# Linear attention and two MLPs on one core: the second MLP's output layer moved to Strassen's scheme

## The chip, the cores and the metric

The kernel runs on one core of a Trainium2 chip. The metric is the device time of one execution in microseconds, the median of several runs; lower is better. Beside the times there is one profiled execution, from which every row below is taken.

## The reference

All data are float32. The attention part and the first MLP come first and are not touched by the change.

```python
q_s = softmax(q, axis=-1); k_s = softmax(k, axis=2)      # 8 batches, 8 heads, 576 positions, 64 wide
x  = (q_s @ (k_s.T @ v)), laid out as 4608 tokens x 512
x  = square(relu(x @ moe_w_in)) @ moe_w_out              # 512 -> 2048 -> 512
h  = x @ moe2_w_in                                       # second MLP: 512 -> 2048
out = (h * sigmoid(1.702 * h)) @ moe2_w_out              # 2048 -> 512
```

## The kernel before

Every float32 matrix operand is cut into a high part (a ScalarE copy that rounds, `to_hi`) and a low part (a subtraction on GpSimd or VectorE, `to_lo`), and each product is three matmuls, hi·hi, hi·lo and lo·hi (`three`). The order of all instructions is written out by hand: a list `ORDER` for the start, and after it a `plan` of steps, each with a time, which is sorted by time. The times only set the order on each engine; semaphores do the rest. SP issues all DMAs, in the order of the plan.

The first MLP runs over 9 blocks of 512 tokens. Its output goes to DRAM (`y_d`). The second MLP runs over 6 blocks of 768 tokens (`NB2`), each block in 8 steps called quads (`NQ`), 256 of the 2048 hidden features per quad.

*First layer of a quad* (`steps_l1`): Strassen's scheme in Winograd's form, so seven products of half-size blocks instead of eight. Each product is 2 chunks x 3 = 6 matmuls with 384 moving columns. The seven forms of x (a11, s2, a12, s3, s1, a22, s4) are made once per block (`steps_s`). The seven forms of w_in live in SBUF for the whole second MLP (tiles w1, wa, wq, wbb, made by `steps_q`). The products accumulate in two PSUM banks (`pa`, `ps`); ScalarE copies the first (m1), VectorE adds m1 to the others (line 815), ScalarE applies the activation (line 824), and `to_hi` (line 134) and `to_lo` (line 137, GpSimd) make the four blocks `gc` of the hidden values.

*Second layer of a quad* (`unit`): plain, 12 units of 3 matmuls with 512 moving columns. The 128 x 128 stationary operand is a piece of the hidden values, the moving operand is a row block of w_out, and the sums of a block's six token tiles stay in six PSUM banks over its 8 quads:

```python
g, w = g_t["2", n, c], wt["o2", i, f]
cs = slice(t * P, (t + 1) * P)
three(acc, lambda e: g[:, e, cs], lambda e: w[:, e, :], len(seen) == 1, len(seen) == NF)
```

The units of quad n-1 stand between the products of quad n:

```python
UNITS = [0, 0, 1, 1, 2, 2, 3, 3, 4, 4, 5, 6]
...
                for e in range(2 if n >= NQ else 0):
                    at(quad(n) + (0.3 + 0.1 * e) * PT, load_o, n // NQ, 2 * (n % NQ) + e)
...
                for e, (c, t) in zip(UNITS, todo, strict=True):
                    at(quad(n) + (e + 0.47) * PT, unit, n - 1, c, t)
```

Two tiles of w_out per quad (512 KB each, hi and lo together) are loaded from DRAM (`wod`, line 712), where block 1 left them (`steps_o`). At the end of a block ScalarE and VectorE copy the banks (lines 899, 901) and six DMAs of 256 KB store 128 rows of 2 KB each (line 903).

Of the kernel before, what the change touches and what calls it, by code (L numbers as in the profile page):

```python
# [53 lines left out]
g15.re x10.s g15.sq g14.hi o15.hi g14.lo x11.s o15.lo x13.xh s13.all x13.xl g15.hi g15.lo  # L54
"""
# [3 lines left out]
def kernel(  # L59
# [54 lines left out]
    PT = QT / 7  # L114
# [28 lines left out]
    def at(t, fn, *args):  # L143
        plan.append((t, len(plan), fn, args))
# [7 lines left out]
    split_d = [dram.tile([P, 2, DM], F32, name=f"wod{f}") for f in range(NF)]  # L152
# [127 lines left out]

    def steps_o(n):
# [9 lines left out]
        def split(e):  # L291
            def run():
                f = 2 * n + e
                w = new_o(0, f)
                to_hi(w[:, 0, :], st["t"][:, e, :])
                to_lo(w[:, 1, :], st["t"][:, e, :], w[:, 0, :], nc.gpsimd)
                nc.sync.dma_start(out=split_d[f], in_=w.bitcast(F32))

            return run

        return dict(ld=load, s0=split(0), s1=split(1))

# [62 lines left out]
    def split_x(i, p):  # L365
# [339 lines left out]
    freed = [(t, f"{kind}{f}") for t, kind, f in freed]  # L705

    def new_o(i, f):
        wt["o2", i, f] = wpool.tile([P, 2, DM], F32R, tag=freed[-4:][f % 4][1], name=f"wo2_{i}_{f}")
        return wt["o2", i, f]

    def load_o(i, f):
        nc.sync.dma_start(out=new_o(i, f).bitcast(F32), in_=split_d[f])

    def steps_s(i):
# [25 lines left out]
        def split(a, src, eng):  # L740
            def run():
                x = xpool.tile([P, 2, 2, TH], F32R, tag=X_AT[a], name=f"{a}_{i}")
                to_hi(x[:, 0], src())
                to_lo(x[:, 1], src(), x[:, 0], eng)
                x_t["2", i, a] = x

            return run

        def s2():
            if i < 2:  # L750
                st["s2"] = block(0, 0)
            else:
                st["s2"] = cpool.tile([P, 2, TH], F32, tag="raw", name=f"s2f{i}")
            sub(st["s2"], st["s1"], block(0, 0), nc.vector if i < 2 else nc.gpsimd)

        def s4():
            sub(block(0, 0), block(0, 1), st["s2"])

        return dict(
            ld=load,  # L760
            s1=s1,
            s3=s3,
            s2=s2,
            a11=split("a11", lambda: block(0, 0), nc.gpsimd),
            s2s=split("s2", lambda: st["s2"], nc.vector),
            a12=split("a12", lambda: block(0, 1), nc.gpsimd),
            s4=s4,
            s3s=split("s3", lambda: block(1, 0), nc.vector),
            s1s=split("s1", lambda: st["s1"], nc.gpsimd),
            a22=split("a22", lambda: block(1, 1), nc.vector),  # L770
            s4s=split("s4", lambda: block(0, 0), nc.gpsimd),
        )

    def steps_l1(n):
# [5 lines left out]
        def product(at, x, begin):  # L780
            def run():
# [3 lines left out]
                w, xs = wt[a, j], x_t["2", i, x]  # L785
# [13 lines left out]
        def tile_(name):  # L799
            pool, tag = dict(  # L800
                m1=(late, "m1"), c12=(late, "c12"), c22=(late, "c22"), c21=(None, "t"), c11=(None, "t")
            )[name]
            pool = cpool if pool is None else late["pool"]
            return pool.tile([P, TH], F32, tag=tag, name=f"{name}_{n}", bufs=2 if tag in ("c12", "t") else 1)
# [23 lines left out]
        def split(name):  # L828
            def run():

                last = (name == "c12") == (n % 2 == 0) and name in ("c12", "c21")
                pool, tag = (late["pool"], "g4") if last else (gpool, "g")
                g = pool.tile([P, 2, TH], F32R, tag=tag, name=f"g{name}_{n}")
                to_hi(g[:, 0, :], st[name])
                to_lo(g[:, 1, :], st[name], g[:, 0, :], nc.gpsimd)
                g_t["2", n, name] = g
# [3 lines left out]
        return [  # L840
            (0.0, product(0, "a11", True)),
            (0.48, m1),
            (1.0, product(1, "s2", True)),
            (1.5, add("c12", 1, "m1")),
            (2.0, product(0, "a12", False)),
            (2.5, act("c11")),
            (3.0, product(1, "s3", False)),
            (3.1, split("c11")),
            (3.5, add("c22", 1, "m1")),
            (4.0, product(0, "s1", True)),  # L850
            (4.5, add("c22", 0, "c22")),
            (4.55, act("c22")),
            (5.0, product(1, "a22", False)),
            (5.1, split("c22")),
            (5.5, add("c21", 1, "m1")),
            (5.55, act("c21")),
            (6.0, product(0, "s4", False)),
            (6.1, split("c21")),
            (6.5, add("c12", 0, "c12")),
            (6.55, act("c12")),  # L860
            (7.1, split("c12")),
        ]

    def unit(n, c, t):

        i, j = divmod(n, NQ)
        if ("2", i) not in acc_t:
            acc_t["2", i] = {}
        tokens = (int(c[1]) - 1) * (NT2 // 2) + t
        f = 2 * j + int(c[2]) - 1  # L870
        if tokens not in acc_t["2", i]:
# [188 lines left out]
```

## Time and profile before

| | |
|---|---|
| median of 3 runs | 1652.45 us (1650.57 to 1653.61) |
| profiled execution, its own time | 1650.79 us |
| its span, first to last instruction | 1649.0 us |
| TensorE busy, share of the span | 99% |
| VectorE, ScalarE, GpSimd busy | 48%, 41%, 41% |
| DMA queue of SP, share of 16 engines | 29.5%, 158.37 MB |

Busy time of TensorE counts overlapping matmuls once. How long a stage takes is read from the start of one product to the start of the same product of the next quad. "PEld" is the load of the stationary operand, which overlaps with the matmul before it.

### The profile page before, as it was taken

What the parts mean: (1) busy time and instruction counts of PE and PEld (TensorE: products, weight loads), DVE (VectorE), ACT (ScalarE), POOL (GpSimd) and SP (SyncE); (2) the same over time, 40 slices, a digit from 0 to 9 for tenths busy, and PEclk for the clock granted to TensorE, in tenths of its full rate; (3) what the DMA queues carried; (4) which work ended last, traced back from release to release, by engine and by line L of the source; (5) the groups of instructions that cost most, each with busy time, mean ns of one, the idle gap of its engine ahead of it and who ended that gap; (6) DMA issues with size and microseconds to landing.
All of it is one profiled execution on the core that took longest, in us unless ns stands there. A gap on an engine that the chain in (4) does not pass through costs nothing.

```text
span 1649.0 us, 21337 instructions
## 1 busy us (share of the span) xinstructions
PE 1629.5 (99%) x7848; PEld 1404.4 (85%) x7848; DVE 789.8 (48%) x1455; ACT 673.2 (41%) x1228; POOL 684.0 (41%) x589
## 2 busy tenths in 40 slices
PE   6999999999999999999999999999999999999999
PEld 5888888888888888888888989889888898898987
DVE  8976777676776767656456113113113113113111
ACT  5874344444444444333435334324234234234332
POOL 4774333433433343343488445234234234234221
PEclk9999999999999999999999999999999999999999
DMA  8742233223323222121312334222222322321212
GB/s 241 236 141 73 73 106 84 81 87 100 100 68 108 82 63 86 61 77 52 103 44 90 141 113 143 90 77 101 104 77 85 120 78 77 128 76 72 96 61 81
DMA packets 127913, 159.74 MB, mean 97 GB/s; under 512 B 54080, under 2 KB 90944, under 8 KB 127808
## 3 DMA queue, kind: packets, MB, share of 16 engines
q1 hardware_dynamic: 127808, 158.37, 29.5%
q8 instruction: 62, 1.02, 0.2%
q14 instruction: 43, 0.35, 0.1%
HBM read 122.68 MB, written 35.65 MB: 96 GB/s over the span
## 4 chain that ended last, share of the span: by engine, by line
PE 91%; DVE 5%; issue 2%; DMA 1%; SPq 1%; ACT 1%; POOL 0%; DVEq 0%; POOLq 0%; ACTq 0%
PE acc L627 45%; PE ph L627 21%; PE ps L627 15%; PE pa L627 6%; PE px L582 2%; PE pk L448 2%; DVE qt L545 1%; DMA rawi<-in_moe_w_in_dram 1%; DVE tpo L206 0%; DVE tpo L203 0%; DVE km L406 0%; DVE tpi L206 0%; DVE tpi L203 0%; DVE to L209 0%; DVE ti L209 0%
## 5 line engine op out<-in xcount | busy, mean ns | idle before, releaser
L627 PE MATMUL acc<-wo,gc 128*128 128x512 f32 x1728 | 453.4, 394 | 0.0
L627 PE MATMUL ph<-x,wi 128*128 128x512 f32 x1728 | 420.8, 392 | 1.8 <-DVE x L137 1.2
L627 PE MATMUL acc<-g,wo 128*128 128x512 f32 x1728 | 419.1, 391 | 0.0
L627 PEld LDWEIGHTS ph<-x,wi 128*128 128x128 f32 x1728 | 321.1, 188 | 69.0 <-DVE x L137 1.5
L627 PEld LDWEIGHTS acc<-g,wo 128*128 128x128 f32 x1728 | 321.8, 188 | 67.2 <-POOL wo L137 0.3
L137 POOL TENSOR_TENSOR gc<-c,gc 128x384 fp32r<-128x384 f32 x192 | 198.2, 1033 | 415.5 <-ACT gc L134 401.5
L627 PEld LDWEIGHTS acc<-wo,gc 128*128 128x128 f32 x1728 | 319.3, 188 | 46.1
L137 POOL TENSOR_TENSOR g<-g,g 128x512 fp32r<-128x512 f32 x144 | 192.2, 1336 | 384.0 <-ACT g L134 347.5
L815 DVE TENSOR_TENSOR c<-ps,m 128x384 f32<-128x384 f32 x144 | 80.2, 557 | 405.7 <-PE ps L627 399.9
L824 ACT ACTIVATE c<-c 128x384 f32<-128x384 f32 x144 | 75.5, 524 | 257.2 <-DVE c L815 257.2
L134 ACT ACTIVATE g<-g 128x512 fp32r<-128x512 f32 x144 | 91.0, 632 | 205.8 <-DVE g L654 205.7
L654 DVE TENSOR_TENSOR g<-g 128x512 f32<-128x512 f32 x128 | 108.0, 843 | 116.5 <-ACT g L648 114.2
L648 ACT ACTIVATE g<-ph 128x512 f32<-128x512 f32 x144 | 85.8, 596 | 163.0 <-PE ph L627 159.9
L545 DVE STREAM_TRANSPOSE qt<-q 32x128 f32<-32x128 f32 x448 | 135.5, 302 | 5.7
L627 PE MATMUL ps<-s,wa 128*128 128x384 f32 x576 | 115.8, 335 | 1.4 <-DVE c L815 1.4
L627 PE MATMUL pa<-a,w 128*128 128x384 f32 x576 | 116.7, 337 | 0.0
L627 PEld LDWEIGHTS ps<-s,wa 128*128 128x128 f32 x576 | 103.0, 188 | 10.2 <-DVE c L815 1.7
L627 PEld LDWEIGHTS pa<-a,w 128*128 128x128 f32 x576 | 103.3, 188 | 9.3 <-ACT m L808 0.8
L815 DVE TENSOR_TENSOR c<-ps,c 128x384 f32<-128x384 f32 x96 | 53.4, 556 | 109.1 <-PE ps L627 109.1
L134 ACT ACTIVATE gc<-c 128x384 fp32r<-128x384 f32 x192 | 100.4, 523 | 9.0 <-POOL wo L137 2.0
L824 ACT ACTIVATE c<-pa 128x384 f32<-128x384 f32 x48 | 23.6, 492 | 175.2 <-PE pa L627 175.2
L627 PE MATMUL ps<-s,wbb 128*128 128x384 f32 x288 | 58.7, 338 | 0.0
(112 smaller groups left out, 1582.2 us busy)
## 6 DMA issues: line engine op xcount, KB each, us to landing
wo<-wod SPq DMA_DIRECT2D x80, 512.0 KB, 4.0
rawi<-in_moe_w_in_dram SPq DMA_DIRECT2D x32, 512.0 KB, 4.5
rawo<-in_moe_w_out_dram SPq DMA_DIRECT2D x32, 512.0 KB, 4.0
y<-o SPq DMA_DIRECT2D x36, 256.0 KB, 2.8
out_dram<-o SPq DMA_DIRECT2D x36, 256.0 KB, 2.0
k<-in_k_dram SPq DMA_DIRECT2D x32, 256.0 KB, 4.3
vt<-in_v_dram SPq DMA_DIRECT2D x64, 128.0 KB, 3.4
wod<-wo SPq DMA_DIRECT2D x16, 512.0 KB, 2.8
```

What stands on the lines that cost most here:

```text
L134: nc.scalar.activation(hi, src, AF.Copy)
L137: eng.tensor_tensor(out=lo, in0=src, in1=hi.bitcast(F32), op=ALU.subtract)
L448: nc.tensor.matmul(st["pk"][:, :VW], st["ke"][:, j, :], st["v"][:, j, :], start=(j == 0), stop=(j == KJ),)
L545: nc.vector.transpose(out=st["qt"][32 * g : 32 * g + 32, a * P : (a + 1) * P].rearrange("d (j t) -> d j t", j=QJ), in_=st["qn"][32 * a : 3 ...
L582: nc.tensor.matmul(st["px"][:, cols], a, c[:, cols], start=(e == 0), stop=(e == 2))
L627: nc.tensor.matmul(out, w(a), x(b), start=(start and e == 0), stop=(stop and e == 2), skip_group_check=shared)
L648: nc.scalar.activation(st["g"], st["h"], AF.Relu)
L654: nc.vector.tensor_tensor(out=st["g"], in0=st["g"], in1=st["g"], op=ALU.mult)
L815: nc.vector.tensor_tensor(out=st[name], in0=st[at][:, :TH], in1=other, op=ALU.add)
L824: nc.scalar.activation(st[name], h, AF.Gelu_apprx_sigmoid)
```

## The change

Block 1 of the second MLP stays as it is. In blocks 2 to 6 the second layer uses Strassen's scheme too, over two quads at a time (a group). The transposed output is built: the stationary operand is now a form of w_out, the moving operand a form of the hidden values with 384 tokens. For each of seven forms and each half t of the output columns there is a `chain` of 2 quads x 3 = 6 matmuls; 14 chains per group, 280 in all. The stationary operand takes every second column of the form (`(d t) -> t d`). One product and one chain alternate (a slot, 2.09 in the plan).

Five forms' chains are added up over the four groups of a block in SBUF (`evict`: ScalarE copy for the first group, VectorE add after), the two others stay in four PSUM banks. At the end of a block `steps_y` makes five VectorE adds of 128x768, four adds from PSUM, eight VectorE transposes of 32x32 squares, and 16 DMAs that store pieces of 64 columns (256 bytes), half of them issued by ScalarE.

Four more combinations of the hidden values are made per quad (VectorE), so seven `to_hi` and `to_lo` per quad instead of four. The forms of w_in and w_out are written to DRAM during block 1 (`keep_in`, `steps_o`, the new `steps_t`) and loaded again for every quad and group: w1, wa and wb have one buffer, wq two, the w_out forms four. Four forms of x are stored in DRAM and loaded again at the end of the block before.

```diff
+    split_i = {(a, j): dram.tile([P, 2, HC if a == "wb" else DM], F32, ...) ...}
+    split_o = {(k, x): dram.tile([P, 2, 2, HC], F32, ...) for k in range(NF // 4) for x in FORMS}
+    split_x = {(i, a): dram.tile([P, 2, 2, TH], F32, ...) ... for a in ("a11", "s2", "a12", "s3")}
...
-    def load_o(i, f):
-        nc.sync.dma_start(out=new_o(i, f).bitcast(F32), in_=split_d[f])
+    W_IN = dict(w1=(3,), wa=(6,), wb=(7,), wq=(8, 9))
+    W_OUT = (10, 11, 12, 13)
...
+    def load_in(n, a):
+        width = HC if a == "wb" else DM
+        w = wpool.tile([P, 2, width], F32R, tag=slots[W_IN[a][n % len(W_IN[a])]], name=f"{a}_{n}")
+        wt["s", a, n] = w
+        nc.sync.dma_start(out=w.bitcast(F32), in_=split_i[a, n % NQ])
+
+    def load_out(k, x):
+        at = (len(FORMS) * k + FORMS.index(x)) % len(W_OUT)
+        w = wpool.tile([P, 2, 2, HC], F32R, tag=slots[W_OUT[at]], name=f"w{x}_{k}")
+        wt["s", x, k] = w
+        nc.sync.dma_start(out=w.bitcast(F32), in_=split_o[k % (NQ // 2), x])
...
+        late_done = max(done(6), done(5) + 2.0)
+            (done(4) + 1.3, "h.a22", hi("a22", "c22")),
+            (done(4) + 1.9, "l.a22", lo("a22", "c22")),
+            (done(5) + 1.3, "s3'", diff("s3", "c11", "c21")),
+            (done(5) + 1.9, "s1'", diff("s1", "c21", "c22", ALU.add)),
+            (done(5) + 2.0, "s2'", diff("s2", "s1", "c11")),
+            (late_done + 1.8, "s4'", diff("s4", "c12", "s2")),
...
+    def chain(c):
+        i, k, at, x, t = chain_of(c)
+        lasting = x in LASTING
+        if not lasting:
+            totals["ps", c] = late_ps["pool"].tile([P, TB], F32, tag=f"acc{4 + c % 2}", ...)
...
+        w = wt["s", x, k].rearrange("p e h (d t) -> p e h t d", t=2)
+        for e in range(2):
+            g = g_t["2", NQ + 2 * k + e, x]
+            three(bank[:, :TH], lambda h: w[:, e, h, t], lambda h: g[:, h, :], ...)
+
+    def evict(c):
...
+        if at == 0:
+            nc.scalar.activation(o, bank, AF.Copy)
+        else:
+            nc.vector.tensor_tensor(out=o, in0=bank, in1=o, op=ALU.add)
...
+        def turn_(x, row, col, t):
...
+                nc.vector.transpose(
+                    st["o"][:, 2 * row + col, :, :, t], both(x)[:, t].rearrange("p (a b) -> p a b", b=32)
+                )
+        def put(row, col, q):
...
+                (nc.sync if q % 2 else nc.scalar).dma_start(
+                    out=out[r0 : r0 + TH, c : c + 64].rearrange("(a b) d -> b a d", b=32),
+                    in_=st["o"][32 * q : 32 * (q + 1), 2 * row + col].rearrange("b a d t -> b a (d t)"),
+                )
...
+        first_half = quad(NQ) + UNITS
+        second_half = first_half + 6 * UT + 4 * PT
+        grid = second_half + 6 * UT
+        SLOT = 2.09
+        last = NQ * (NB2 - 1) * 7 - 11
+        def product_at(n, e):
...
+            at = 7 * (n - NQ - 1) + e - 4
+            return first_half + 6 * UT + PT * e if at < 0 else grid + SLOT * at
+        def chain_at(c):
+            return grid + SLOT * min(c, last) + PT * (1 + max(c - last, 0))
...
+                for a, e in (("w1", 2), ("wa", 4), ("wb", 6), ("wq", -1)):
+                    t = product_at(n - 1, e) + PT + 0.1 if e >= 0 else product_at(n - 1, 0) + 0.5
...
+                at_y = dict(u2=7, u3=7.1, c21=7.2, o100=7.3, o101=7.4, c22=9, u4=9.2, o110=9.4, o111=9.6)
+                at_y.update(c120=10, c121=11, o010=10.5, o011=11.5, c110=12, c111=13, o000=12.5, o001=13.5)
```

In `at_y` the number counts the chains of the block's last group; u2 to c22 are the adds, c11 and c12 the adds from PSUM, o the transposes. The two lines shown are those of the last block.

## Rows read from the trace of the kernel before

**Rows 1.** Part 1 of the page: busy time, share, instructions per engine.
```profile
PE 1629.5 (99%) x7848; PEld 1404.4 (85%) x7848; DVE 789.8 (48%) x1455; ACT 673.2 (41%) x1228; POOL 684.0 (41%) x589
```

**Rows 2.** Windows: stretch, length, busy per engine, TensorE clock, DMA share, GB/s.
```profile
1099.90:1115.58 15.68, 15.68 (x79) 14.10 (x78) 2.79 (x5) 4.66 (x9) 7.69 (x6) 1.00 0.18 68
1010.00:1626.80 616.80, 616.80 (x3068) 554.27 (x3067) 136.98 (x229) 210.28 (x398) 217.13 (x188) 1.00 0.25 93
```

**Rows 3.** Timeline of TensorE in one quad: start, length of the merged stretch.
```profile
1099.90 1.21 PE L627 MATMUL ps<-a,wq 128*128 128x384 f32 x6
1100.94 0.86 PE L627 MATMUL acc<-wo,gc 128*128 128x512 f32 x3
...
1106.89 1.55 PE L627 MATMUL acc<-wo,gc 128*128 128x512 f32 x6
1108.28 1.21 PE L627 MATMUL pa<-a,w 128*128 128x384 f32 x6
```

**Rows 4.** Timeline of TensorE around the start of the second MLP.
```profile
892.19 1.33 PE L627 MATMUL ps<-s,wa 128*128 128x384 f32 x6 [1.36 <-DVE c L815]
...
896.12 1.23 PE L627 MATMUL ps<-s,wa 128*128 128x384 f32 x6
...
900.31 1.55 PE L627 MATMUL acc<-wo,gc 128*128 128x512 f32 x6
```

**Rows 5.** Timeline of TensorE's loads and matmuls with 130 columns.
```profile
691.47 1.31 PEld L448 LDWEIGHTS pk<-vt,ke 128*128 128x128 f32 x10
```

**Rows 6.** Line 191, ScalarE reading every second word; line 134, reading every word.
```profile
L191 ACT ACTIVATE to<-rawo x32: 633/652/676, 31.2 to 786.5; 128x512 f32<-128x512 f32 x32
L134 ACT ACTIVATE x<-xf x31: 614/633/635, 122.9 to 795.0; 128x512 fp32r<-128x512 f32 x31
```

**Rows 7.** Groups of instructions by line from 800 us: busy, mean ns, idle before.
```profile
L137 POOL TENSOR_TENSOR gc<-c,gc 128x384 fp32r<-128x384 f32 x192 | 198.2, 1033 | 415.5 <-ACT gc L134 401.5 <-issue 8.5 <-PE acc L627 5.4
L134 ACT ACTIVATE gc<-c 128x384 fp32r<-128x384 f32 x192 | 100.4, 523 | 9.0 <-POOL wo L137 2.0
L815 DVE TENSOR_TENSOR c<-ps,m 128x384 f32<-128x384 f32 x144 | 80.2, 557 | 405.7 <-PE ps L627 399.9 <-POOL xf L731 4.1 <-ACT m L808 1.6
L824 ACT ACTIVATE c<-c 128x384 f32<-128x384 f32 x144 | 75.5, 524 | 257.2 <-DVE c L815 257.2
L808 ACT ACTIVATE m<-pa 128x384 f32<-128x384 f32 x48 | 23.4, 487 | 3.0
L137 POOL TENSOR_TENSOR s<-s1f,s 128x768 fp32r<-128x768 f32 x6 | 11.8, 1968 | 10.9 <-ACT s L134 10.9
```

**Rows 8.** Lines 545, 654, 327, 731 on VectorE: duration ns min/median/max.
```profile
L545 DVE STREAM_TRANSPOSE qt<-q x448: 289/303/309, 142.8 to 784.0; 32x128 f32<-32x128 f32 x150
L654 DVE TENSOR_TENSOR g<-g x128: 670/693/2331, 133.1 to 882.7; 128x512 f32<-128x512 f32 x128
L327 DVE TENSOR_TENSOR tb<-tt,tb x8: 424/428/1399, 807.6 to 902.2; 128x256 f32<-128x256 f32 x8
L731 DVE TENSOR_TENSOR xf<-xf,s2f x4: 951/954/954, 1124.6 to 1501.1; 128x768 f32<-128x768 f32 x4
L731 DVE TENSOR_TENSOR xf<-s1f,xf x2: 958/1503/2048, 849.9 to 998.2; 128x768 f32<-128x768 f32 x2
```

**Rows 9.** Timelines of VectorE and GpSimd at the same moment.
```profile
842.64 1.76 DVE L319 TENSOR_TENSOR ta<-tt 128x512 f32<-128x512 f32 x1 [3.33 <-POOL wa L137]
...
842.56 1.29 POOL L137 TENSOR_TENSOR wq<-tb,wq 128x512 fp32r<-128x512 f32 x1
...
863.04 0.68 DVE L319 TENSOR_TENSOR ta<-tt 128x512 f32<-128x512 f32 x1
```

**Rows 10.** Windows with the densest DMA, columns as in rows 2.
```profile
1151.00:1160.00 9.00, 9.00 (x46) 8.00 (x45) 1.93 (x4) 2.45 (x6) 3.04 (x3) 1.00 0.92 328
1159.00:1160.00 1.00, 1.00 (x6) 0.79 (x6) 0.56 (x1) 0.00 (x0) 0.00 (x0) 1.00 1.07 416
40.00:48.00 8.00, 8.00 (x44) 6.75 (x43) 7.55 (x13) 6.81 (x14) 5.22 (x6) 1.00 1.03 326
```

**Rows 11.** DMA issues: count, KB of one, median us to landing.
```profile
wo<-wod SPq DMA_DIRECT2D x80, 512.0 KB, 4.0
```

**Rows 12.** Lines 394 and 903: ns that SP takes to issue a DMA.
```profile
L394 SPq DMA_DIRECT2D vt<-in_v_dram x64: 549/607/631, 6.8 to 662.2; - x64
L903 SPq DMA_DIRECT2D out_dram<-o x36: 332/333/367, 1019.2 to 1645.7; - x36
```

**Rows 13.** Timeline of the end.
```profile
1636.05 9.04 PE L627 MATMUL acc<-wo,gc 128*128 128x512 f32 x39
...
1645.12 0.60 ACT L899 ACTIVATE o<-acc 128x512 f32<-128x512 f32 x1 [0.76 <-PE acc L627]
```

More of the change, by code (lines that the diff above doesn't have):

```diff
@@ L55 @@
 """
+CHANGE = """
+"""
 @with_exitstack
@@ L740, in split, with hi @@
         def split(a, src, eng):
[L741 to L747, printed above, removed]
+            def hi():
+                if i and a in ("a11", "s2", "a12", "s3"):
+                    st["x", a] = [wpool.tile([P, 2, TH], F32R, tag=slots[4 + e], name=f"{a}{e}_{i}") for e in range(2)]
+                else:
+                    st["x", a] = xpool.tile([P, 2, 2, TH], F32R, tag=X_AT[a], name=f"{a}_{i}")
+                    st["x", a] = [st["x", a], st["x", a][:, 0], st["x", a][:, 1]]
+                to_hi(st["x", a][-2], src())
@@ new lines, in lo, with again @@
+            def lo():
+                *x, hi_, lo_ = st["x", a]
+                to_lo(lo_, src(), hi_, eng)
+                if x:
+                    x_t["2", i, a] = x[0]
+                    return
+                for e in range(2):
+                    nc.sync.dma_start(out=split_x[i, a][:, e], in_=st["x", a][e].bitcast(F32))
+            def again():
+                x = x_t["2", i, a] = xpool.tile([P, 2, 2, TH], F32R, tag=X_AT[a], name=f"{a}_{i}")
+                nc.sync.dma_start(out=x.bitcast(F32), in_=split_x[i, a])
@@ L749, in s2 @@
+            steps = {f"h.{a}": hi, f"l.{a}": lo}
+            if i and a in ("a11", "s2", "a12", "s3"):
+                steps[f"r.{a}"] = again
+            return steps
         def s2():
-            if i < 2:
-                st["s2"] = block(0, 0)
-            else:
[L753 to L772, printed above, removed]
+            sub(block(0, 0), st["s1"], block(0, 0))
@@ new lines, in s4 @@
+        def s4():
+            if i:
+                sub(block(0, 1), block(0, 1), block(0, 0))
+            else:
+                sub(block(0, 0), block(0, 1), block(0, 0))
+        steps = dict(ld=load, s1=s1, s3=s3, s2=s2, s4=s4)
+        for a, src, eng in (
+            ("a11", lambda: block(0, 0), nc.gpsimd),
+            ("s2", lambda: block(0, 0), nc.vector),
+            ("a12", lambda: block(0, 1), nc.gpsimd),
+            ("s3", lambda: block(1, 0), nc.vector),
+            ("s1", lambda: st["s1"], nc.gpsimd),
+            ("a22", lambda: block(1, 1), nc.vector),
+            ("s4", lambda: block(0, 1) if i else block(0, 0), nc.gpsimd),
+        ):
+            steps.update(split(a, src, eng))
@@ L826, in act, with diff @@
             return run
-        def split(name):
+        def diff(out, a, b, op=ALU.subtract):
             def run():
-                last = (name == "c12") == (n % 2 == 0) and name in ("c12", "c21")
-                pool, tag = (late["pool"], "g4") if last else (gpool, "g")
-                g = pool.tile([P, 2, TH], F32R, tag=tag, name=f"g{name}_{n}")
+                if out in ("s3", "s4"):
+                    st[out] = tile_(out)
+                else:
+                    st[out] = st[dict(s1="c21", s2="c11")[out]]
+                nc.vector.tensor_tensor(out=st[out], in0=st[a], in1=st[b], op=op)
+            return run
@@ L834, in run, with hi, lo @@
+        def hi(x, name):
+            def run():
+                if i:
+                    g = g_tile(x, n)
+                else:
+                    last = (name == "c12") == (n % 2 == 0) and name in ("c12", "c21")
+                    pool, tag = (late["pool"], "g4") if last else (gpool, "g")
+                    g = pool.tile([P, 2, TH], F32R, tag=tag, name=f"g{name}_{n}")
+                st["g", x] = g
                 to_hi(g[:, 0, :], st[name])
+            return run
+        def lo(x, name):
+            def run():
+                g = st["g", x]
```

402 lines of the change are left out of this document (293 added, 109 removed).

## The prediction

> **What bounds the kernel now.** I read the page's first part, then the second MLP's quads in a table of windows, then single matmuls in the timeline. TensorE is busy for 99% of the span [rows 1], and from 1010 to 1626.8 us for all of it [rows 2]. A quad repeats every 15.68 us, with VectorE busy for 2.79, ScalarE 4.66, GpSimd 7.69 us and DMA at 0.18 of its time [rows 2]. So TensorE alone sets the pace and everything else has room. What counts is columns: a product of six 384-column matmuls takes 1.04 us from start to start, six 512-column ones 1.39 us [rows 3], 0.45 ns a column both times, so no fixed price per matmul.
>
> **What the change removes on TensorE.** A quad has 42 matmuls of 384 and 36 of 512 columns, 34,560 in 15.68 us, 0.4537 ns each. Afterwards it has 42 + 42 of 384, 32,256 columns, 14.63 us. That is 1.05 us less, 40 times: **41.8 us**. Whether 384-column matmuls can follow each other without a 512-column one between, whose length gives the weight load more time: rows 4 show four products in a row, 24 matmuls from 896.12 to 900.31, 1.05 us per product. They can. I also need the loads to be no dearer with every second column. No load in the trace does that. The nearest are loads of adjacent columns between 130-column matmuls, ten in 1.31 us, 0.13 us apiece [rows 5], so there are 0.04 us to spare in a 0.174 us matmul. ScalarE reads every second word at 652 ns against 633 [rows 6]. I price the stride at nothing; the other end is twice the load, which is a rival below.
>
> The Trainium skill's page "SBUF — State Buffer", section "Door 1: The DMA port swizzle", says that accesses are free of loss while at least two fall into each 16-byte line. Two 4-byte words 8 bytes apart do; the sum by the page is the same, and it is a reason to keep that rival's chance small.
>
> **What the other engines get.** Per quad: ScalarE seven roundings of 0.523, four activations of 0.524 and one copy of 0.487, 6.2 us, and 8.7 in a block's first group, when it also copies five chains. GpSimd has seven subtractions of 1.033, 7.2 us [rows 7]. VectorE has five adds of 0.557 [rows 7], five evictions of the same form, and four sums in SBUF. For those: 256 elements take 0.428, 512 take 0.69 [rows 8], so 384 some 0.56 us. A VectorE operation with both inputs in SBUF, however, waits while GpSimd is at work: at 842.64 one takes 1.76 us, begun with a GpSimd one of 1.29, and 0.68 where it stands free [rows 9]. GpSimd being busy half the time, I take 0.85, so 5 x 0.557 x 2 + 4 x 0.85 = 9 us. All this fits under 14.63; I price it at nothing as a mean. In block 1 the new w_out forms, sums and stores fall under 15.68 us quads whose other engines are half idle, also nothing; were GpSimd late there, the forms would miss only their first load.
>
> *Order at block ends.* GpSimd also makes the low part of x's s1, 1.968 us [rows 7], placed 1.2 after the fifth product of the block's last quad, ahead of the a22 subtraction (1.03). The latter ends at 1.2 + 1.97 + 1.03 = 4.2 us, when its chain is due at 4.18 (two slots after). With semaphores I take 0.6 us late, at four boundaries: **2.4 us**. Ends: 0, and 5.2 if both run beside VectorE.
>
> *Where the schemes meet* seven products and then four run with nothing between them to cover the PSUM drains. Where the second MLP starts now one product waited 1.36 us for a VectorE add [rows 4]. I take **1.0 us**, ends 0 and 3.
>
> **DMA.** A tile is 512 KB [rows 11], 0.524 MB. Per quad: w1, wa, wq and half of one for wb, 3.5 tiles, and 3.5 of w_out: 3.67 MB where there were two tiles. A block of eight quads: 29.4 MB, four x forms of 0.79 MB written and read (6.3), the first MLP's output in (1.6) and the result out (1.6): 38.8 MB in 117 us. What the DMA engines can do, worked out as GB/s over share [rows 10]: 328/0.92 = 357 over 9 us of such loads; 416 over the best 1 us; 326/1.03 = 317 where small pieces mix in. So a block takes 109 us of its 117: hidden as a mean, with little left. At a block's end it is not even: the last two quads ask 7.3 for weights, 3.1 to load x forms and half of their stores, 1.6, together 12.1 MB, 33.8 us in 29.3: 4.5 us behind. SP, which issues in order, also holds later loads some 2 us while an x store waits for its subtraction. That makes 6.5. What gives first is w1, with one buffer: free after its quad's third product, needed five slots on, 10.45 - 1.04 - 4.0 to land [rows 11] = 5.4 us of slack. Late by 1.1 us, four times: **4.4 us**. At 416 GB/s nothing is late. At 317 the two quads take 38.2 us, 8.9 behind and 10.9 with SP's hold, 5.5 late, 22 us in all.
>
> The window's best microsecond, 416 GB/s, lies above what the Trainium skill's page "DMA: Bandwidth & Descriptors", section "Specifications", gives as a core's share of the memory, about 358 GB/s; the nine-microsecond row lies at it. By the page a block takes 108 us and the sum is mine; by the single row, 93 us, and the sum is that of the first rival.
>
> **The tail.** Now the last matmul ends at 1645.09 and the span 3.9 us later [rows 13]. After the change, the last chains run without products between them and VectorE cannot follow. From the end of the last group's eighth chain it has three evictions (1.7), five adds of 128x768 at 0.954 (4.8) [rows 8], four adds from PSUM at 0.557 (2.2) and eight transposes. One of 128 elements takes 0.303 [rows 8], 256 more cost 0.26 by the adds' slope, 0.57 each, 4.6 (upper end three times 0.303, 0.91). Together 13.3 us, while six chains take 6.3: VectorE ends 7.0 after the last matmul. Then what follows the last copy today, 1649.0 - 1645.72 = 3.3, and the last four stores on two queues, two of 0.607 instead of one of 0.333 [rows 12], 0.9. That is 11.2 against 3.9: **7.3 us** lost. Ends: 2, if VectorE needs only its last add, transpose and issues, and 10 with 0.91.
>
> **Sum.** 41.8 - 2.4 - 1.0 - 4.4 - 7.3 = 26.7 us. The profiled execution took 1650.79 us for a span of 1649.0 and gives 1624.1; on the median of the runs, 1652.45, it is 1625.8. I say **1626**.
>
> **Rivals.**
>
> *DMA keeps up.* The loads run near 400 GB/s, and the queue order costs nothing. For it: 416 in rows 10, nothing but large pieces in the weight streams. Against it: only 1 us long, and no stretch has writes of small pieces among them. 41.8 - 7.3 - 1.0 = 33.5: 1619 us (1611 to 1621.5). Chance 0.27.
>
> *DMA becomes the bound.* At 317 GB/s a block needs 122 us, more than TensorE's 117. For it: the result leaves in 256-byte pieces, reads and writes alternate, 40 to 48 us is such a mixture. Against it: the stream is mostly 4 KB rows. 41.8 - 7.3 - 1.0 - 2.4 - 22 = 9.1: 1643 us (1634 to 1649). Chance 0.18.
>
> *The strided weight load*, on the other side. In the chains 40 x 42 = 1680 loads take every second column. Above 0.174 us each nanosecond costs 1.7 us; 26.7 us are used up at 0.19 us. At twice the 0.13 of rows 5, 0.26, a chain takes 1.56 instead of 1.04 us, 280 x 0.52 = 146 us lost: about 1770. For it: 0.13 leaves little room. Against it: rows 6. Chance 0.08.
>
> *VectorE becomes the bound around block ends.* In the twelve slots, 25 us, of a block's closing sums it has 10 us of ordinary work, 2.2 from PSUM, 4.6 to 7.3 of transposes and five large adds at 0.954 to 2.05 [rows 8], 4.8 to 10.2: 22 to 30 us. At the upper end products wait 5 us for their adds, 20 us in all on top of the forecast: 1646, with the longer transposes past 1650. For it: the long row of 2048 ns. Against it: the mean of the others. Chance 0.05.
>
> **How the numbers follow.** The forecast's own case has 0.42 and 1621.5 to 1634. The range 1611 to 1644 leaves out the strided load (0.08), the busy VectorE (0.05) and about 0.05 of the DMA case: 0.82 inside. Faster by over 0.2% (3.3 us, about what a measurement of this kernel can tell from no change): 0.27 + 0.42 + 0.17 = 0.86. Within it 0.04, from the upper end of the DMA and VectorE cases. Slower 0.10: the strided load and the rest of those. That TensorE's work is not what the change says is excluded by the code; the count of 1680 matmuls with 384 columns in the chains would show it.
>
> **What the profile afterwards should show.** Right: a quad of blocks 2 to 6 at 14.6 us inside a block; chains at 1.04 us, weight loads 188 ns in both kinds; DMA share 0.7 early in a block and near 1 in its last two quads; a TensorE wait of about 1 us for a w1 or wa load at each of four boundaries; 11 us from the last matmul to the end, with VectorE busy. Wrong: chains longer than products (stride), waits for DMA in every quad (bound), waits for VectorE adds in the third to fifth product of a block's first quads (VectorE), or a tail of 6 us.

## The result, and the profile after

The changed kernel takes 1638.75 us (median of 4 runs, 1636.38 to 1640.52). The kernel before took 1651.93 in runs beside it (1650.57 to 1653.61). The ratio is 0.9919 [0.9902, 0.9936]: 13.2 us are gained where 26.7 were summed, and the time lies inside the forecast's range. The profiled execution took 1640.52 us, the longest of the four, for a span of 1638.4, 10.6 us below the span of before.

The page's first part, to be read beside [rows 1]:

```profile
PE 1600.5 (98%) x8088; PEld 1431.8 (87%) x8088; DVE 1062.8 (65%) x1871; ACT 739.7 (45%) x1399; POOL 851.0 (52%) x721
```

TensorE has 29 us less to do, yet it now stands idle for 38 us of the span instead of 19.5. The table of windows shows where; columns as in [rows 2].

```profile
995.00:1011.00 16.00, 15.34 (x76) 13.47 (x75) 2.74 (x5) 6.35 (x14) 7.79 (x7) 1.00 0.86 311
1016.40:1018.70 2.30, 2.23 (x7) 2.23 (x8) 0.56 (x1) 0.01 (x1) 2.30 (x3) 0.54 0.82 237
1040.00:1580.00 540.00, 532.08 (x3009) 526.78 (x3008) 354.72 (x548) 249.37 (x512) 338.70 (x281) 1.00 0.93 322
1100.00:1114.63 14.63, 14.63 (x86) 14.63 (x85) 9.61 (x17) 6.58 (x13) 8.99 (x9) 1.00 0.84 299
1114.63:1129.26 14.63, 14.63 (x85) 14.63 (x84) 9.60 (x14) 7.39 (x15) 9.22 (x8) 1.00 0.95 345
1620.00:1638.40 18.40, 7.52 (x44) 7.21 (x42) 12.89 (x21) 0.00 (x0) 0.15 (x1) 0.80 0.49 114
```

Inside a block TensorE is busy throughout and the granted clock is full, 1.00 of 2.4 GHz. VectorE's 9.6 us a quad and GpSimd's 9.1 leave room. DMA is another matter: 0.93 of its time over most of the five blocks, 322 GB/s, where [rows 2] had 0.25 and 93. The last window, after the chains run out, is the tail. The second window lies where the schemes meet: there the granted clock is 0.54, nearly all of it at the lower level, 1.2 GHz.

The timeline of TensorE at four places: where the schemes meet, three changes of scheme inside a block, the end of block 2, and the end of the kernel.

```profile
1011.24 1.23 PE L681 MATMUL pa<-a,w 128*128 128x384 f32 x6
1014.39 1.32 PE L681 MATMUL ps<-s,wq 128*128 128x384 f32 x6 [1.93 <-DVE c L905]
1016.47 2.22 PE L681 MATMUL pa<-a,w 128*128 128x384 f32 x6 [0.76 <-ACT m L898]
...
1046.79 1.23 PE L681 MATMUL pa<-a,w 128*128 128x384 f32 x6
1047.86 1.20 PE L681 MATMUL pcs<-gs,ws 128*128 128x384 f32 x6
1048.90 1.23 PE L681 MATMUL ps<-s,wa 128*128 128x384 f32 x6
...
1131.10 1.20 PE L681 MATMUL pca<-ga,wa 128*128 128x384 f32 x6
1133.29 1.30 PE L681 MATMUL pa<-a,w 128*128 128x384 f32 x6 [0.99 <-DMA w<-wiw]
...
1623.20 2.24 PE L681 MATMUL pls<-gs,ws 128*128 128x384 f32 x12
1625.28 2.24 PE L681 MATMUL pla<-ga,wa 128*128 128x384 f32 x12
```

Three things are to be seen. A chain that follows a product starts 1.07 us after it (1046.79 to 1047.86), a product that follows a chain 1.04; two chains in a row take 2.08 (1623.20 to 1625.28), no more than two products. Within such a pair the time is lost inside the product: the six matmuls of the product at 1048.90 start 0.175, 0.177, 0.185, 0.176 and 0.182 us apart, those of the chain before it 0.173 or 0.174. The block's end costs 1.15 us for a load of w1 (1131.10 + 1.04 to 1133.29). And the meeting of the schemes has two waits, of 1.93 and 0.76, after which TensorE runs at the lower clock (the product at 1016.47 takes 2.22 us, the one at 1011.24 1.23).

All waits of TensorE from 1010 us on (engine and line, released by: us in total, times, longest):

```profile
PE ps L681 <- DVE c L905: 2.6, 3, 1.9
PE pcs L681 <- ACT sums L1081: 1.9, 4, 1.0
PE pa L681 <- DMA w<-wiw: 1.8, 2, 1.0
PE pa L681 <- DVE c L905: 1.7, 1, 1.7
PE pa L681 <- DVE c L924: 0.8, 1, 0.8
PE pa L681 <- ACT m L898: 0.8, 1, 0.8
PE ps L681 <- DMA wa<-wiwa: 0.7, 2, 0.6
PE pcs L681 <- DVE suma L1083: 0.6, 2, 0.5
```

These are 11 us, and none is put down to GpSimd. The lost time as a whole I take from the starts of the matmuls: from the start of block 2's first product (1011.24) to the end of the last matmul, each start is set against the one before plus a matmul's time (0.174 us for 384 columns); what is over in a step of up to 0.12 us counts as a small gap, more as a large one. Records that are missing make each line uncertain by about 1 us.

| profiled execution | us lost | in the forecast |
|---|---|---|
| block 2 starts later (1011.24 against 1009.28) | 2.0 | 0 |
| gaps in the first 26 us, where the schemes meet | 4.8 | 1.0 |
| small gaps in the blocks | 7.3 | 0 |
| large gaps in the blocks | 11.9 | 2.4 + 4.4 |
| tail, last matmul to the end, 10.9 against 3.9 | 7.0 | 7.3 |

About 1.5 of the 4.8 us where the schemes meet are the lower clock: ten matmuls between 1016.9 and 1019.8 start 0.32 us apart instead of 0.174.

The kernel before has 1.7 us of such gaps too, so 33.0 - 1.7 = 31.3 of the 41.8 us are lost, and 10.5 remain.

### The profile page after: what moved, and what is told of

Same layout as the page of the kernel before. It is cut to its first block, busy times and chain, and to the rows that moved or that the text cites. A ratio compares the mean times of both kernels' runs of the same rounds, so it can differ in the third digit from the quotient of the medians.

```text
span 1638.4 us, 23452 instructions
## 1 busy us (share of the span) xinstructions
PE 1600.5 (98%) x8088; PEld 1431.8 (87%) x8088; DVE 1062.8 (65%) x1871; ACT 739.7 (45%) x1399; POOL 851.0 (52%) x721
## 5 line engine op out<-in xcount | busy, mean ns | idle before, releaser
L143 POOL TENSOR_TENSOR ga<-c,ga 128x384 fp32r<-128x384 f32 x120 | 130.3, 1088 | 127.9 <-ACT ga L140 95.7
L681 PE MATMUL pcs<-gs,ws 128*128 128x384 f32 x720 | 144.5, 337 | 2.8 <-ACT sums L1081 1.9
L143 POOL TENSOR_TENSOR gs<-s,gs 128x384 fp32r<-128x384 f32 x80 | 99.4, 1243 | 69.2 <-ACT gs L140 64.7
L681 PEld LDWEIGHTS pcs<-gs,ws 128*128 128x128 f32 x720 | 126.9, 194 | 5.8 <-ACT sums L1081 4.4
L143 POOL TENSOR_TENSOR gs<-c,gs 128x384 fp32r<-128x384 f32 x80 | 93.2, 1180 | 12.1 <-ACT gs L140 6.8
L681 PE MATMUL pca<-ga,wa 128*128 128x384 f32 x480 | 95.8, 336 | 0.0
L681 PEld LDWEIGHTS pca<-ga,wa 128*128 128x128 f32 x480 | 85.0, 194 | 0.0
```

Source lines behind the costliest of these rows:

```text
L143: eng.tensor_tensor(out=lo, in0=src, in1=hi.bitcast(F32), op=ALU.subtract)
L681: nc.tensor.matmul(out, w(a), x(b), start=(start and e == 0), stop=(stop and e == 2), skip_group_check=shared)
```

## The experiments

The first eight of these kernels ran beside runs of the kernel before of 1650.85 us, the last four beside runs of 1651.56. Each starts from the changed kernel. Since the runs beside them differ, kernels are best compared by the ratio to the kernel before; the change has 0.9919 [0.9902, 0.9936], and where an interval overlaps with that one, a difference of a few us is not shown. One profile can mislead by as much: the stretch where the schemes meet lost 2.9 us in one kernel and 6.0 in another (stores from SP, adds on GpSimd), although neither edit touches it.

**Where the schemes meet: the load of w_out's last tile earlier.** ScalarE's timeline in the changed kernel shows what its activations stood behind:

```profile
1009.26 0.63 ACT L140 ACTIVATE wo<-to 128x512 fp32r<-128x512 f32 x1 [6.47 <-DMA to<-wod]
```

It stood 6.47 us behind the load `to`. In the same kernel's queue of SP that load is issued behind two loads of x forms:

```profile
999.94 0.65 SPq L835 DMA_DIRECT2D a<-xa  x1
1000.68 1.44 SPq L835 DMA_DIRECT2D s<-xs  x1
1002.17 0.93 SPq L310 DMA_DIRECT2D to<-wod  x2
```

```diff
-            times = (...)[n] if n < 2 else (2.0, 4.3, 5.7)
+            times = (...)[n] if n < 2 else ((0.05 if n == NQ - 1 else 2.0), 4.3, 5.7)
```

> Moved: the load of the last pair of w_out rows for block 1 (the tile to) is issued at the start of block 1's last quad, ahead of two reloads of x forms, instead of behind them. Theory (the 4.8 us lost where the schemes meet come from ScalarE standing 6.5 us behind that load in its order): the seven products of block 2's first quad run without a gap, ScalarE's wait of 6.5 us falls under 2 us, and the time falls by 4 to 5 us, to about 1634. Rival (the gaps come from the PSUM drains themselves, as nothing stands between the products): the wait of ScalarE goes, but the gaps of about 4 us stay and the time is unchanged, 1638 to 1639.

Measured: 1640.75 us, 0.9936 [0.9923, 0.9948], no gain. The wait itself went, as TensorE's timeline of this kernel shows (0.23 instead of 1.93; the 0.76 stayed):

```profile
1013.28 1.32 PE L681 MATMUL ps<-s,wq 128*128 128x384 f32 x6 [0.23 <-DVE c L905]
1015.36 1.34 PE L681 MATMUL pa<-a,w 128*128 128x384 f32 x6 [0.76 <-ACT m L898]
```

The granted clock now stays full there: the product behind the 0.76 takes 1.34 us where it took 2.22. The gaps where the schemes meet fell from 4.8 to 1.6 us, some 1.7 by the wait and 1.5 by the clock; the large gaps in the blocks rose from 11.9 to 14.6. So the cause of the wait is right, and the number that I gave for its removal is not: by these profiles, what TensorE wins there it waits for later.

**Stores of the result from SP alone.** ScalarE's timeline in the changed kernel, at a wait of TensorE for a line 1081 copy at 1417.80:

```profile
1415.26 1.95 ACTq L1111 DMA_DIRECT2D out_dram<-o  x2
1417.25 0.49 ACT L1081 ACTIVATE sums<-pcs 128x384 f32<-128x384 f32 x1 [2.87 <-DMA out_dram<-o]
```

The 1.95 us are two issues and the time between them, and the copy that frees a chain's PSUM bank stood behind both. The issues themselves are short, as the view of that line shows (ns min/median/max):

```profile
L1111 ACTq DMA_DIRECT2D out_dram<-o x40: 322/354/877, 1164.6 to 1634.4; - x40
```

These two took 0.32 us each. The second waits on a semaphore that it shares with a load of w1, issued by SP at 1410.6: that load landed at 1416.86, the store was issued at 1416.88. So ScalarE is held by late DMAs, and hands the delay on to the chains.

```diff
-                (nc.sync if q % 2 else nc.scalar).dma_start(
+                nc.sync.dma_start(
```

> Changed: all 16 stores of a block's result are issued by SP, none by ScalarE. Theory (TensorE's waits for evictions by ScalarE, some 3 us in all, come from ScalarE being held while it issues stores): these waits vanish and the time falls by 2 to 3 us, to about 1636. Rival (SP is the scarcer queue: each store holds the loads of weights behind it): the waits for evictions vanish, new waits for weight loads come in their place, and the time is unchanged or up to 5 us longer.

Measured: 1636.24 us, 0.9909 [0.9896, 0.9923], 2.5 us below the change by the medians, 1.6 by the ratios, with intervals that overlap. No wait for line 1081 is left, so that part of the theory is right; how much time it gives is not shown. Those for w1 and for VectorE's differences have grown (1.8 to 2.3, 0.8 to 1.8):

```profile
PE pa L681 <- DMA w<-wiw: 2.3, 2, 1.4
PE pa L681 <- DVE c L924: 1.8, 2, 1.2
```

**Half of the loads of w_in's forms.** Every second quad uses the forms of the quad before.

```diff
     def load_in(n, a):
+        if n % 2:
+            wt["s", a, n] = wt["s", a, n - 1]
+            return
```

> Left out: every second quad of blocks 2 to 6 uses the w_in forms of the quad before instead of loading its own, so half of the w_in stream (36.7 of about 190 MB from block 2 on) is not moved, and those quads compute with the wrong forms. Theory (TensorE waits for late loads only at the four block ends, 6 us in all): the DMA share in the blocks falls from 0.92 to 0.97 to about 0.7, the 6 us and no more come back, about 1633. Rival (a nearly full DMA system delays all the rest too, through ScalarE and SP): 12 us or more come back, 1627 or less. If DMA costs nothing: no change, 1639.

Measured: 1632.6 us, 0.9887 [0.9872, 0.9903], 6.2 us below the change (5.3 by the ratios; the intervals just touch). The window of the five blocks has DMA at 0.79:

```profile
1040.00:1580.00 540.00, 537.37 (x3049) 533.97 (x3048) 358.69 (x558) 253.63 (x521) 340.52 (x284) 1.00 0.79 265
```

Large gaps are 5.2 us instead of 11.9, small ones as before (6.9). So some 6 us of the loss wait for DMA, as the theory said, and the small gaps have another cause.

**Chains that take adjacent columns.** Only the view in `chain` changes, so that each half of the columns is put out at the wrong place.

```diff
-        w = wt["s", x, k].rearrange("p e h (d t) -> p e h t d", t=2)
+        w = wt["s", x, k].rearrange("p e h (t d) -> p e h t d", t=2)
```

> Changed: the chains' stationary operand takes 128 adjacent columns instead of every second one, so that the output's columns come out permuted. Theory (a product followed by a chain takes 2.11 us instead of 2.08 for a reason that has nothing to do with the stride, since 12 strided matmuls in a row at the end take 2.08): no change, slot 2.11 us and 1638 to 1639. Rival (the strided load costs 6 ns more, 194 against 188 in the records, and with it 0.02 us per slot): slot 2.08 us, and the time falls by about 5 us, to 1633.

Measured: 1637.42 us, 0.9918 [0.9905, 0.9932]. The timeline of TensorE now has product and chain 1.04 us apart in both orders:

```profile
1046.32 1.20 PE L681 MATMUL pcs<-gs,ws 128*128 128x384 f32 x6
1047.36 1.20 PE L681 MATMUL ps<-s,wa 128*128 128x384 f32 x6
1048.40 1.20 PE L681 MATMUL pcs<-gs,ws 128*128 128x384 f32 x6
```

The mean load of a chain's weights went from 194 to 188 ns in the groups by line, first of the changed kernel:

```profile
L681 PEld LDWEIGHTS pcs<-gs,ws 128*128 128x128 f32 x720 | 126.9, 194 | 5.8 <-ACT sums L1081 4.4
```

then of this one:

```profile
L681 PEld LDWEIGHTS pcs<-gs,ws 128*128 128x128 f32 x720 | 126.0, 188 | 6.9 <-ACT sums L1081 5.5
```

Small gaps fell from 7.3 to 0.8 us: the stride costs 6.5 us. My theory here, that it costs nothing, is refuted. But large gaps rose from 11.9 to 15.6, and the ratio is that of the change. About 1.5 us of the rise are the clock again: after a wait of 2.30 us for w1 the window from 1133.6 to 1136.9 has a granted clock of 0.50.

**Two products, then two chains.** Half as many changes between the schemes.

```diff
-            return first_half + 6 * UT + PT * e if at < 0 else grid + SLOT * at
+            return ... if at < 0 else grid + SLOT * (at - at % 2) + PT * (at % 2)
...
-            return grid + SLOT * min(c, last) + PT * (1 + max(c - last, 0))
+            m = min(c, last)
+            return grid + SLOT * (m - m % 2) + PT * (2 + m % 2 + max(c - last, 0))
```

> Changed: the order on TensorE inside blocks 2 to 6 is two products, then two chains, instead of one and one; all instructions stay. The run with adjacent columns took away 6.5 of the 7.3 us of small gaps. Theory (the small gap belongs to the first strided load behind a product, so it comes once per change from product to chain): the small gaps halve to 3.5 to 4 us, and the time falls by 0 to 4 us. Rival (each strided load costs its 6 ns, whatever stands before): the small gaps stay at 7 us and the time stays at 1638 to 1639.

Measured: 1642.72 us, 0.9955 [0.9941, 0.9970], slower than the change. TensorE's timeline:

```profile
1046.25 2.24 PE L681 MATMUL pcs<-gs,ws 128*128 128x384 f32 x12
1048.33 2.27 PE L681 MATMUL ps<-s,wa 128*128 128x384 f32 x12
1050.44 1.90 PE L681 MATMUL pcs<-gs,ws 128*128 128x384 f32 x10
```

Two chains take 2.08, two products with the change to the next chain 2.11: the price is one of 0.03 us for each change from one kind to the other and back, not one for each strided load. The starts of the matmuls say at which change: the first product of a pair, the one behind a chain, is 0.027 us longer in the mean, the second, the one ahead of a chain, 0.001. So it is not the first strided load behind a product that is late, as the theory has it, but the product behind strided loads; the count is the same. Small gaps are 3.3 us, half of before. Large gaps are about 18 instead of 11.9. One wait of 2.5 us, at 1374.75, is put down to one of VectorE's evictions (line 1083), but the load of w1 landed at the same moment, within 0.01 us, and behind the wait the granted clock is 0.50 from 1374.6 to 1378.0, some 1.4 us more. The order by ones is the better one; why the order in pairs has more of the large gaps stays open.

**The last block's closing adds on GpSimd.** Three of the five adds of the last block move to GpSimd and the fourth combination is made before the block c22, which is therefore computed from a combination that has already been changed.

```diff
-            return lambda: nc.vector.tensor_tensor(out=both(out), ...)
+            eng = nc.gpsimd if i == NB2 - 1 and (out, x) in (("s2", "a11"), ("s3", "s2"), ("a22", "s3")) else nc.vector
+            return lambda: eng.tensor_tensor(out=both(out), ...)
...
```

> Moved: of the last block's five closing adds three go from VectorE to GpSimd, and the transposes are ordered by what is ready first. Theory (from the last matmul on the end is VectorE's queue, 10.9 us against 3.9): VectorE has 2.9 us less to do, the tail falls to 8 to 9.5 us and the time by 1.5 to 3 us, to about 1636.5. Rival (the tail is the way of the last stores, 3.9 us to land and two queues of eight): the tail stays at 10.5 to 11 us.

Measured: 1644.19 us, 0.9962 [0.9949, 0.9975], and a tail of 13.0 us instead of 10.9. On GpSimd's timeline the adds take 1.83 and 2.42 us, where VectorE had 0.96:

```profile
1625.42 1.83 POOL L1092 TENSOR_TENSOR sums<-suma,sums 128x768 f32<-128x768 f32 x1 [1.80 <-DVE sums L1083]
...
1629.24 2.42 POOL L1092 TENSOR_TENSOR suma<-sums,suma 128x768 f32<-128x768 f32 x1
```

They depend on each other, so VectorE waits for the last. A VectorE add that overlaps with them took 2.45 instead of 0.96, as in [rows 9]. The tail is a chain, and a slower engine in it only makes it longer. It explains 2.1 us of the median's 5.4; the rest of this profile's excess lies in gaps before the last block, which the edit does not touch.

**Two x forms that don't go through DRAM.** s2 and s3 of the next block are computed straight into their buffers when those come free (after the second and fourth product of the last quad) instead of being stored and loaded again. That takes 3.1 of 38.8 MB per block off the queues.

```diff
-                if i and a in ("a11", "s2", "a12", "s3"):
+                if i and a in ("a11", "a12"):
...
-                    times += [on(6, 3.0), on(6, 4.0), e(1) + 0.2]
+                    times += [e(1) + 0.4, e(1) + 1.2]
```

> Changed: two of the four x forms, s2 and s3, are cut into high and low part at the end of the block before, from the tile that is still there, instead of being stored in DRAM and loaded again; 3.1 of 38.8 MB per block are not moved. Theory (the waits at the block ends, some 6 us, are for loads that come late because the DMA engines are behind): the first product of each block comes without its wait of 1 to 1.9 us, 3 to 5 us fewer in all, about 1634.5. Rival (VectorE and ScalarE are the scarcer at that place): the waits stay, now for VectorE, and the time is 1638 to 1642.

Measured: 1628.26 us, 0.9865 [0.9850, 0.9879], 10.5 us below the change (8.9 by the ratios), about twice what was expected of it. All its waits of TensorE from 1010 us on:

```profile
PE pcs L681 <- ACT sums L1081: 1.8, 3, 1.0
PE pa L681 <- ACT m L898: 0.8, 1, 0.8
PE pcs L681 <- DVE suma L1083: 0.6, 2, 0.5
PE ps L681 <- DVE c L905: 0.4, 2, 0.2
```

None is for DMA or for VectorE at a block's end, and the gaps where the schemes meet are 1.6 us: of the two loads ahead of `to` the second is gone, and DMA in the 16 us before 1011 fell from 0.86 to 0.56. Over the five blocks its share fell only from 0.93 to 0.89. The place of these transfers, at the block's end and ahead of the loads with the least slack, counts for more than their bytes: the experiment with half the loads took three times as much off the mean share and gained 6 us. But the edit takes away two things at once. In the changed kernel SP, which issues in order, also stood behind these forms, as its waits from 1150 to 1560 us show:

```profile
SPq L835 <- DMA xs<-s: 16.6, 4, 5.7
```

Before it may load s3 it waits until its store has landed, and the loads of weights behind it are issued that much later. How much of the gain is due to the bytes and how much to this hold, no run separates.

**Columns put in order when the forms are made.** The step that writes w_out's forms in block 1 writes the even columns first, so that chains load adjacent columns and the output is the same.

```diff
+    def by_half(t): return t.rearrange("p (c d t) -> p c t d", c=2, t=2)
+    def adjacent(t): return t.rearrange("p (c t d) -> p c t d", c=2, t=2)
-                to_hi(w[:, 0, :], st["t"][:, e, :])
+                to_hi(adjacent(w[:, 0, :]), by_half(st["t"][:, e, :]))
```

> Changed: the forms of w_out are written with even and odd columns apart when they are made in block 1, so that the chains load 128 adjacent columns and the output stays as it was; block 1's result is put back in order when it is copied from PSUM. Theory (as in the run with adjacent columns: 6.5 us of small gaps go, part of it is given back in waits for DMA): small gaps under 1.5 us, waits at block ends longer by 2 to 4 us, time 1636 to 1637.5. Rival (the strided reads and writes in block 1 hold ScalarE, GpSimd and VectorE up): block 1 gets longer by 2 us or more and the time is 1639 or more.

Measured: 1637.39 us, 0.9926 [0.9910, 0.9943]. Small gaps are 0.7 us and large ones 13.8, much as with adjacent columns alone. The time is in the expected range, and its interval holds the change's ratio too.

**More DMA.** After each load of wb the same 256 KB are copied once more within DRAM, and nobody waits for it.

```diff
+        if a == "wb":
+            nc.sync.dma_start(out=dram.tile([P, 2, HC], F32, ...), in_=split_i["wb", n % NQ])
```

> Added: behind each load of a wb form the same 256 KB are copied from DRAM to a spare place in DRAM that nobody reads, 40 times, about 0.7 us of all DMA engines per quad. Theory (the DMA engines are all but full, 0.93 in the blocks, and what they are late by is waited for at the block ends): the share goes to 0.96 or more and the time grows by 8 to 25 us, to 1647 to 1664. Rival (the waits at the block ends are a matter of order and latency, not of how full the engines are): the time grows by under 4 us.

Measured: 1642.95 us, 0.9951 [0.9933, 0.9968], 4 to 5 us above the change, with intervals that just overlap. In its window from 1040 to 1580 us the DMA share is 0.96 and 339 GB/s. The number lies between what the theory and the rival gave, and its profiled span, 1637.6, is no longer than the change's. It decides nothing, except that the queues still took 5% more bytes.

**All together.** Four of these edits in one kernel: x in place, columns in order, stores from SP, the `to` load early.

> All together: s2 and s3 of x cut in place, w_out forms with even and odd columns apart, all stores by SP, the last w_out rows of block 1 loaded ahead of the x forms. Theory (with the DMA engines relieved, what is saved on TensorE is no longer given back): the 6 us of small gaps and most of the 4.7 us of waits that the run with x in place still had go, time 1619 to 1623. Rival (the engines are full again as TensorE gets faster): 1625 to 1628.

Measured: 1619.16 us (1617.13 to 1619.73), 0.9803 [0.9788, 0.9817], 19.6 us below the change. From 1040 to 1580 us TensorE is busy for 539.35 of 540 us, with DMA at 0.90. All its waits of TensorE from 1010 us on:

```profile
PE ps L687 <- DVE c L911: 0.8, 3, 0.4
PE pa L687 <- ACT m L904: 0.8, 1, 0.8
PE pcs L687 <- DVE suma L1089: 0.6, 2, 0.5
```

From the start of block 2's first product to the end of the last matmul it takes 595.3 us where the kernel before takes 635.8: 40.5 of the 41.8 us of columns. What is left of the loss is the tail, 11.0.

**The same without the columns in order.**

> As the run with all together, but the chains load every second column as in the changed kernel. Theory: the small gaps of 6.5 us stay, the waits for evictions (2.5 us in the run with x in place) go: 1625 to 1627, 5 to 7 us above the run with all together. Rival (the engines are full): no difference between the two.

Measured: 1625.52 us, 0.9844 [0.9829, 0.9858]: 6.4 us above the kernel with all of them, with intervals far apart. Here the stride costs what the small gaps say, where with DMA as in the change its removal gave nothing that the ratios can tell.

**x in place and half of the loads of w_in's forms.**

> Left out: every second quad of blocks 2 to 6 computes with the w_in forms of the quad before; also s2 and s3 of x cut in place. Theory (with x in place nothing waits for DMA any more): the DMA share falls from 0.89 to about 0.75 and the time is that of x in place alone, 1627 to 1629. Rival (DMA still costs): 1624 or less.

Measured: 1627.89 us, 0.9861 [0.9845, 0.9878], against 0.9865 [0.9850, 0.9879] with x in place alone. In its window the DMA share is 0.73:

```profile
1040.00:1580.00 540.00, 539.59 (x3067) 538.11 (x3068) 355.94 (x561) 254.22 (x520) 338.52 (x285) 1.00 0.73 241
```

That is 0.16 below x in place alone, and the medians show no gain: with x in place no more time waits for DMA than a measurement can tell.

## Why the prediction was half right

The measured 1638.75 us lies inside the stated range, but 12.7 us above the forecast: half of the 26.7 us came. The range was wide enough for losses that the sum did not have, so the hit owes something to luck.

**The columns, 41.8 us: right.** 384-column matmuls follow each other at 0.174 us, a quad takes 14.6 to 14.8 us, and the kernel with all the edits gets 40.5 of it between the two ends of the Strassen blocks.

**The strided load, priced at nothing: the step that failed.** It costs 6.5 us, 0.024 for each of some 270 changes between chain and product. The rival named the cause and mis-sized it by a factor of twenty: it let every strided load cost, where chains run at full pace and only the product behind a chain is late, at its fourth and sixth matmul most of all. The sign that the prediction gave, chains longer than products, is the wrong way round. Why the delay falls there stays open. The nearest row, ScalarE's strided read at 652 against 633 ns [rows 6], was 3% dearer, and 194 against 188 ns for the load is 3% too. That the two have one cause is not shown, but the row was a reason not to price the stride at nothing.

The Trainium skill's page "SBUF — State Buffer", section "Door 1: The DMA port swizzle", names no loss where two accesses fall into a 16-byte line. Here the runs show 194 against 188 ns and 6.5 us, and the measurement decides.

**Where the schemes meet, 1.0 us: mis-sized, and for a reason that the prediction did not have.** It is 4.8, and 2.0 more before it (of which 0.66 is a TensorE wait for w_out's low part, line 143 on GpSimd; the rest is not settled). I looked at PSUM and VectorE; what was late was ScalarE, 6.47 us behind a load queued behind two loads of x, and about 1.5 us were the lower clock behind the two waits, which the prediction did not think of. Block 1 was priced at nothing because its engines were half idle. DMA there was not: 0.86 in its last 16 us. With the load issued earlier, or x kept in place, the gaps are 1.6.

**DMA at the block ends, 4.4 us: right, 4.9 and 1.0 more.** A block's mean share came out at 0.93, which is also what 109 of 117 us gives, though the rate at a full queue was 322/0.93 = 346 GB/s where 357 was taken. The first product of blocks 3 to 6 waits, as forecast, for w1: 1.15 us at 1133.29, 1.87 at 1254.35, 0.97 at 1374.71 and 0.94 at 1495.74, together 4.9. The view of waits puts the second and third down to VectorE, but in all four the load of w1 landed last, 0.09 to 0.14 us before the product. Two waits for wa, at 1261.44 and 1381.41, add 1.0. The views of the DMA issues (count, KB each, median us to landing) of the whole run and of 1244.0 to 1244.5 us:

```profile
w<-wiw SPq DMA_DIRECT2D x40, 512.0 KB, 5.4
w<-wiw SPq DMA_DIRECT2D x1, 512.0 KB, 10.2
```

A 512 KB load takes 5.4 us in the median, not the 4.0 of [rows 11] on which the slack of 5.4 rested, and the four loads at the block ends took 9.0, 10.2, 9.2 and 9.3. The hold of SP behind an x store, taken as 2 us, is 4.2 in the mean. What I did not say is that a nearly full queue can take back what is won elsewhere: the early `to` load and the adjacent columns removed 3.2 and 6.5 us of gaps and gave nothing clear in the time. The rival in which DMA is the bound had the measured time in its interval, but not its mechanism: fewer loads in every quad give 6 us, and with x in place none.

**GpSimd's order at block ends, 2.4 us: not seen.** No TensorE wait from block 2 on is put down to GpSimd. In its place stood a wait that the sum did not have: ScalarE issues half of the stores, its issues wait for earlier DMAs to land, and chains wait for the copies behind them, 3.2 us in all by the starts of the matmuls. The stores were counted for the tail alone, not for the four block ends before it. That 2.4 and 3.2 are close is chance.

**The tail, 7.3 us: right at 7.0.** VectorE's last operations in the changed kernel:

```profile
1628.75 1.03 DVE L1102 STREAM_TRANSPOSE o<-sums 128x384 f32<-128x384 f32 x2
...
1633.42 0.58 DVE L1102 STREAM_TRANSPOSE o<-suma 128x384 f32<-128x384 f32 x1
```

It ends at 1634.00, 6.5 us after the last matmul (7.0 forecast), and the span ends 4.4 later (4.2). A transpose of 384 takes 0.58 us alone and some 0.52 in a pair, where 0.57 was taken.

Put together, 6.5 for the stride, 4.8 + 2.0 - 1.0 for the meeting and block 1, and 11.9 - 6.8 for large gaps make 17.4 us above the forecast; less the 1.7 of before and 0.3 at the tail, 15.4, where the span is 1638.4 - (1649.0 - 26.7) = 16.1 above. With the stride, the x forms, the stores and the `to` load put right, the kernel comes to 1619.16, the number of the rival in which DMA keeps up; it moves 3.1 MB per block less, so this does not bear that rival out.

## What to carry to other kernels

Price a change that fills the DMA queue by the loads with the least slack and by what stands ahead of them in the queue, not by the mean share; taking 8% of the bytes away at a block's end, and with them a hold of the issuing queue, gave 10.5 us here, a fifth of the bytes elsewhere 6. When an edit removes a wait and the time doesn't move, sum the gaps by kind before you call the cause wrong: the strided load cost the same 6.5 us of small gaps in both cases, which did not show in the time beside a nearly full queue and showed as 6.4 once it was relieved. Read what ended an engine's idle time before you price an issue: a merged stretch holds waits too. An engine that issues DMAs and also clears PSUM hands the lateness of the DMAs on. After a long wait of TensorE, look at the granted clock, which made two of these waits 1.4 to 1.5 us dearer.

## What the runs showed of the hardware

- Weight loads of every second 4-byte column took 194 ns where loads of adjacent columns took 188. Chains with such loads ran at full pace (12 matmuls in 2.08 us); the product of adjacent loads behind a chain took 1.07 us instead of 1.04.
- ScalarE took 0.32 to 0.88 us to issue a store of 96 KB in 256-byte pieces, median 0.35; but at 1415.26 two such issues held it for 1.95 us, since the second waited until a load with the same semaphore had landed.
- A load of 512 KB landed 4.0 us after its issue in the median at a DMA share of 0.25, 5.4 at 0.93, and 9.0 to 10.2 at the block ends.
- TensorE's granted clock fell to 0.50 after waits of 1.93 and 0.76 us (changed kernel, from 1016.57 us on, for 3.3 us), of 2.30 (adjacent columns) and of 2.53 us (two and two). With waits of 0.23 and 0.76 in the first place it stayed at 1.00, and so it did after one of 2.25 us (columns in order).
- In the run with more DMA the 16 DMA engines together took 339 GB/s at a share of 0.96 for 540 us, with loads of 512 KB, stores of small pieces and copies within DRAM side by side.
- Three dependent adds of 128x768 on GpSimd took 1.83 to 2.42 us each; VectorE's took 0.96, and 2.45 where the two engines worked at once.
